# A recurrence with chunked preparation: ScalarE's copy of the decay product moves behind the scan, preparation is spread anew, and all preparations of the prologue stand ahead of the turning of the inverse

## The chip, the cores and the metric

The kernel runs on one core of one Trainium2 chip, in one launch. The metric is the device time of a launch in microseconds (us). An engine executes its own instructions strictly in the order in which the program gives them, and waits at an instruction until what it reads is there. So where an instruction stands in an engine's order is as much a part of the kernel as what it computes.

## What is computed

The first part is a linear recurrence for 32 heads (4 batches of 8) over 768 time steps, with a state of 40 x 40 for each head. The second part is a small mixture of attention experts that reads the recurrence's output `x`.

```
for t in range(768):                                  # state: (4, 8, 40, 40), zero at first
    y[t]  = einsum('bhd,bhde->bhe', r[t], state)
    Sa    = einsum('bhde,bhe->bhd', state, a[t])
    state = state * w[t][:, :, None, :] - einsum('bhd,bhe->bhde', Sa, b[t])
    state = state + einsum('bhd,bhe->bhde', v[t], k[t])
x = y as (4, 768, 320)
# for each of 4 experts: q, k, v = x @ wq, x @ wk, x @ wv; causal softmax attention; @ wo;
# out += (the expert's gate, if it is one of the token's two best) * that
```

All tensors are float32; `w` lies between 0.85 and 0.95.

## The kernel before, in words

**Tiling.** The 768 steps are cut into 24 chunks of 32 steps. The heads are cut into 4 groups of 8. A unit is one chunk of one group, so there are 96 units. Four chunks make a block (the code's `w` or `W`, 0 to 5), that is 16 units.

**Preparation.** For every block and group there is one preparation (`prep(i)`, i = 4W + group, 0 to 23), on tiles of 104 partitions. Its parts have one-letter names, and the tables that set the order use them:
- `a`: VectorE scans the decays backward, which gives their products from each step to the chunk's end (tile SUF, L248; the odd ones of groups 1 to 5 go to a part of TT).
- `b`: ScalarE copies four of these products, the decay over the whole stretch, to PC (L250). They are needed much later, when the state crosses into the next block (L413).
- `c`, `s`: VectorE's reciprocal (L252) and its second, forward scan (SC, L254).
- `x`: a multiply that gives AA (L256). `k`, `l`: VectorE's two multiplies that give KB (L261); `p` is the same on GpSimd in one instruction (L258), and only the prologue uses it.
- `m`, `n`: 32 small matmuls each on TensorE (L275) and the masked evacuation to GL by VectorE (L278). `o`: the DMA that puts a part of GL into DRAM (Ld, L282).
- `d`, `q`: AA copied into GL, by ScalarE for the first eight preparations, by VectorE for the others (L265, L267).
- `w`, `v`, `e`: the loads of the next preparation's inputs into EW, EA, EK.

**Inverse.** Each block needs the inverse of triangular matrices of 32 x 32 (`invert`): `L` loads them from Ld to MT, `C` sets the diagonal, `T5` does five of the elimination's instructions (L309), `A`, `B`, `D`, `E` turn the result by VectorE's transpose into TT (L311). It runs on GpSimd, 60 instructions a block. For block 0 it runs on VectorE with 28 instructions in the prologue (`T28`), then `P` turns a part into P1 (L313), and `F0`, `H0` to `F3`, `H3` finish it on TensorE and ScalarE, one chunk at a time (L320, L328).

**The loop.** It has 100 steps n, each with seven places in a fixed order: `u` of unit n-1 (L382, L384), `g` of unit n (L373, L376), `y` of unit n-3 (the state product, L405, L415; on VectorE at a block's end, L413), `f` of unit n-2 (L395, L398), `t` (L431, L435), `k` (L362, L366), `v` of unit n-1 (L389, L390). The decay multiply of the step (L419) stands behind the jobs of the place `f`. A unit's chain goes from TensorE to ScalarE or VectorE and back at each place, and its state is needed again four steps later by the same group.

**What sets the order.** START is the prologue, ahead of the loop. EARLY, SIDE, SIDE2 and INV add jobs to the loop's steps: the key is the step relative to 16(W-1), and the slashes count the seven places, so that `"///0abc"` puts a, b and c of the block's group 0 behind place 3, `f`. SIDE2 stands in for SIDE for block 2, which starts three steps later because EARLY still finishes block 1 in the first steps. In the kernel before, START prepares groups 0 to 4 fully and groups 5 and 6 in part ahead of `T28`; the parts of 5 to 7 that are left stand behind `F0` or in EARLY.

**Buffers.** In the prologue the inputs of preparations 1 to 7 lie in tiles that the loop needs only later (E8). SUF is one tile, so a next scan overwrites it only when `b`, `p` or `k`, `l` of the one before have read it.

Of the kernel before, what the change touches and what calls it, by code (L numbers as in the profile page):

```python
# [22 lines left out]
EARLY = {
    0: "///6cs",
    1: "5mno///6x 7apb/F1",
    2: "6mno///7csx/H1",
    3: "7mno E8",
    4: "/F2/5d/5q",
    5: "/H2/6d/6q",
    6: "/F3/7d/7q",  # L30
    7: "/H3",
}

SIDE = {
    -16: "///0abc",
    -15: "///0sx///0wv",
    -14: "///0k",
    -13: "///0l 1abc///0e",
    -12: "///0m 1s///1w",
    -11: "///1xkl///1ve",  # L40
    -10: "///2abc 1m",
    -9: "///2sx///2wv",
    -8: "///2kl///2e",
    -7: "///3abc 2m",
    -6: "///3sx///3wv",
    -5: "///3k",
    -4: "///3l 0ndqo///3e",
    -3: "///3m 1ndqo",
    -2: "///2ndqo",
    -1: "///3ndqo",  # L50
}

SIDE2 = {
    -13: "///0abc",
    -12: "///0sx///0wv",
    -11: "///0kl 1abc///0e",
    -10: "///1sx///1wv",
    -9: "///0m 1kl///1e",
    -8: "///2abc 1m",
    -7: "///2sxk///2wv",  # L60
    -6: "///2l 3abc///2e",
    -5: "///2m 3sx///3wv",
    -4: "///3kl 0ndqo///3e",
    -3: "///3m 1ndqo",
    -2: "///2ndqo",
    -1: "///3ndqo",
}
# [903 lines left out]
```

## Time and profile before

| what | value |
|---|---|
| median of 3 runs | 684.5 us (683.43 to 689.24) |
| the profiled execution's own time | 682.19 us |
| its span in the profile | 680.0 us |
| TensorE matmul, busy | 593.9 us (87%) |
| VectorE (DVE), busy | 493.1 us (73%) |
| ScalarE (ACT), busy | 474.3 us (70%) |
| GpSimd (POOL), busy | 321.0 us (47%) |

PE is TensorE's matmul and PEld its weight load. A time like 218.06 is counted from the span's start. In the rows of the timeline the first number is the start, the second the duration of the row's instructions together, and the bracket behind gives how long the engine sat idle just before and what ended that. Whole-span shares hide stages with different limits, so the stretches of the recurrence are looked at one by one. The first state product of chunks 4, 8, 12, 16 and 20 starts at 152.9, 215.1, 278.8, 337.6 and 379.6 us; these are the stretches' borders.

### The profile page before, as it was taken

To read this page: it belongs to the slowest core of one execution; us is meant where nothing else is said; L and a number is where in the kernel's file an instruction comes from. 1 tells how busy PE (TensorE), PEld (TensorE's weight loads), DVE (VectorE), ACT (ScalarE), POOL (GpSimd) and SP (SyncE) were. 2 spreads that over 40 slices of the span, in tenths; PEclk is the share of its full clock that TensorE was granted. 3 is DMA by queue.
4 is the path that set the end of the run, shared out by engine and by line. 5 is a ranking of instruction groups with operands and counts; after the bars stand their busy time and mean duration, and the time that the engine had idled before them with its cause. 6 is when DMAs were issued, how large, how long until landed. Compare 5 with 4: busy or idle time off the path is not lost. (4 is left out here: it accounts for less than half of the span.)

```text
span 680.0 us, 23382 instructions
## 1 busy us (share of the span) xinstructions
PE 593.9 (87%) x9361; PEld 514.6 (76%) x9361; DVE 493.1 (73%) x1164; ACT 474.3 (70%) x1295; POOL 321.0 (47%) x456
## 2 busy tenths in 40 slices
PE   5538797987997998889999989889899989999995
PEld 5527686976886887778988777778778877887774
DVE  7687458787887788788757776668887587667651
ACT  6892376666876786778899998457576666676762
POOL 2312089529925980797286020135555255343731
PEclk8555659788899799899999999989999999999998
DMA  7750445445655455653633882522131213202101
GB/s 240 221 124 11 105 126 120 103 119 151 153 128 157 129 135 115 181 131 87 174 97 83 259 211 69 165 56 73 56 92 35 78 32 83 65 11 57 40 30 46
DMA packets 63693, 73.90 MB, mean 109 GB/s; under 512 B 30168, under 2 KB 48344, under 8 KB 63576
## 3 DMA queue, kind: packets, MB, share of 16 engines
q1 hardware_dynamic: 63432, 72.21, 40.5%
q8 instruction: 77, 1.26, 0.8%
q14 instruction: 40, 0.33, 0.2%
q10 hardware_dynamic: 144, 0.10, 0.0%
HBM read 54.99 MB, written 11.01 MB: 97 GB/s over the span
## 5 line engine op out<-in xcount | busy, mean ns | idle before, releaser
L820 POOL TENSOR_TENSOR P<-P,m 128x128 f32<-128x128 f32 (+2 forms) x96 | 87.6, 934 | 95.3 <-DVE m L816 49.4
L309 POOL TENSOR_TENSOR MT<-MT,TP 128x30 f32<-128x30 f32 (+9 forms) x150 | 97.6, 651 | 11.8
L405 PE MATMUL py<-R,LS 128*40 128x80 f32 x1536 | 89.9, 246 | 14.9 <-ACT LS L435 9.7
L309 POOL TENSOR_TENSOR TP<-MT 128x30 f32<-128x30 f32 (+9 forms) x150 | 93.6, 624 | 11.4
L398 DVE TENSOR_TENSOR R<-ps,CM 64x128 f32<-64x128 f32 x192 | 55.1, 287 | 45.7 <-PE ps L395 42.2
L405 PEld LDWEIGHTS py<-R,LS 128*40 128x40 f32 x1536 | 67.4, 124 | 24.3 <-ACT LS L435 16.5
L809 ACT ACTIVATE P<-sc,m 128x128 f32<-128x128 f32 (+2 forms) x96 | 60.8, 634 | 29.9 <-DVE m L808 23.5
L275 PE MATMUL ps<-AA,KB 40*64 40x32 f32 x1536 | 64.2, 244 | 19.4 <-DVE AA L256 14.0
L275 PEld LDWEIGHTS ps<-AA,KB 40*64 40x64 f32 x1536 | 60.3, 164 | 23.0 <-issue 18.7
L808 DVE TENSOR_REDUCE m<-sc 128x1 f32<-128x128 f32 (+2 forms) x96 | 59.4, 622 | 20.1 <-PE sc L801 18.8
L798 PE MATMUL sc<-ks,qs 128*128 128x384 f32 (+4 forms) x256 | 62.5, 345 | 5.3 <-ACT P L809 5.1
L376 ACT ACTIVATE GT<-ps 32x160 f32<-32x160 f32 x192 | 56.4, 294 | 14.2 <-PE ps L373 10.8
L395 PE MATMUL ps<-RB,VU 128*64 128x64 f32 x768 | 49.3, 238 | 13.7 <-ACT VU L390 13.5
L384 ACT ACTIVATE R<-ps 32x160 f32<-32x160 f32 x192 | 56.6, 295 | 5.4 <-PE ps L382 1.2
L395 PEld LDWEIGHTS ps<-RB,VU 128*64 128x64 f32 x768 | 39.1, 148 | 19.5 <-ACT VU L390 18.5
L828 PE MATMUL pt<-CM,P 128*128 128x128 f32 x336 | 51.9, 276 | 2.1 <-ACT pt L834 1.8
L366 ACT ACTIVATE LS<-pt 64x320 f32<-64x320 f32 x96 | 41.4, 432 | 15.9 <-PE pt L362 14.5
L435 ACT ACTIVATE LS<-pt 40x320 f32<-40x320 f32 x92 | 39.6, 430 | 15.7 <-PE pt L431 12.6
L382 PE MATMUL ps<-GT,TT 128*33 128x80 f32 x768 | 48.8, 252 | 1.8 <-ACT GT L376 0.9
L798 PEld LDWEIGHTS sc<-ks,qs 128*128 128x128 f32 x256 | 40.8, 190 | 10.5 <-ACT P L809 9.4
L720 PE MATMUL pt<-xh,wq 128*128 128x384 f32 x192 | 43.3, 361 | 2.8 <-DVE pt L832 1.2
L431 PE MATMUL pt<-CM,R 104*104 104x104 f32 x368 | 44.6, 266 | 0.2 <-issue 0.2
(154 smaller groups left out, 1314.0 us busy)
## 6 DMA issues: line engine op xcount, KB each, us to landing
RB<-in_RB SPq DMA_DIRECT2D x24, 320.0 KB
EK<-in_EK SPq DMA_DIRECT2D x18, 416.0 KB
ks<-ks SPq DMA_DIRECT2D x32, 192.0 KB
R<-in_VG SPq DMA_DIRECT2D x24, 208.0 KB
EA<-in_EA SPq DMA_DIRECT2D x19, 208.0 KB
EW<-in_EA SPq DMA_DIRECT2D x18, 214.5 KB
R<-in_VT SPq DMA_DIRECT2D x48, 80.0 KB
R<-in_RT SPq DMA_DIRECT2D x24, 160.0 KB
```

The costliest lines, as they stand in the source:

```text
L275: T.matmul(p_a[64 * s:64 * s + 64, p, cc - c], kb[q, n, :], aa[q, n, :], start=True, stop=True, tile_position=(64 * s, 64 * s))
L309: return [lambda: e.tensor_tensor(tmp, row, col, op=OP.mult), lambda: e.tensor_tensor(o, o, tmp, op=OP.add)]
L376: A.activation(gt[b:b + 32, s::2], p_g[64 * s:64 * s + 32], AF.Copy)
L384: A.activation(hd(r2[32:64, 40 * h0:40 * h0 + 320], 80)[:, x::2], p_u[64 * x:64 * x + 32], AF.Copy, scale=-1.0)
L395: T.matmul(p_f[64 * x:64 * x + 64, y], vu[:, p, :], rb[:, 4 * g + p, :], start=True, stop=True, tile_position=(0, 64 * x))
L398: V.tensor_tensor(o[:, :, x], p_f[64 * x:64 * x + 64], mask[x][:, None, None, :].to_broadcast([64, 2, 2, 32]), op=OP.mult)
L405: T.matmul(py[64 * s:64 * s + 40, p], ls[:, h, :], m, start=True, stop=True, tile_position=(0, 64 * s))
L798: T.matmul(ps[:, c, 0:cw], QS[b][:, e, o], KS[b][:, e, z, k], start=(z == 0), stop=(z == 1 and not last), skip_group_check=True)
L808: V.tensor_reduce(m[:, 0, t:t + 1], ps[:, 0:ch, 0:cw], axis=AX.XY, op=OP.max, negate=True)
L809: later(DE, lambda: A.activation(pv, ps[:, 0:ch, 0:cw], AF.Exp, bias=m[:, 0, t:t + 1], accum_out=m[:, 1, t:t + 1]))
L820: PL.tensor_tensor(P[:, 0:n], P[:, 0:n], m[:, 3, t:t + 1].to_broadcast([128, n]), op=OP.mult)
L828: T.transpose(p[:, 128 * y:128 * y + 128], st["P"][t][:, 128 * c:128 * c + 128], ident)
```

## The change

- START is written anew. All eight preparations of blocks 0 and 1 stand ahead of `A B P F0 H0`. Their `m n o` stand behind the next group's `a` (and for groups 0 to 2 behind `csx` of the next as well), and `b` stands some way behind `a` and not right after it. Preparation 1 makes KB on VectorE. `T28` is cut into two `T14` with group 7's `m n o` between them.
- EARLY keeps `F1` to `H3` alone, at other steps.
- SIDE has `b` two or three steps behind `a`, at most three parts of a preparation in a step, and the copies `d q` are taken out of steps -4 to -1 and put into steps 1, 3, 6 and 8, when the block before runs. SIDE2 and INV1 are gone: all blocks use SIDE and INV. INV starts `C` and `T5` in the step of `L`.
- RB1 and P1 no longer have memory of their own; they lie in TT of block 1. Input tiles of preparation 7 lie elsewhere, and its SUF is the one in TT.

```diff
-START = """Z0 E4 0abcsxkl E5 E7 E6 1apb 0m 0d 0q 0n 0o 1csx W2 2apb 1m 1d 1q 1n 1o W4 2csx 3apb 2m 2d 2q 2n 2o W0 W1 V00 V10
-3csx 4apb 3m 3d 3q 3n 3o L W3 4csx W5 W6 5apbc 4m 4n C V01 V11 k0 g0 4o Z1 4d 4q T28 A B P F0 5s H0 5x 6apb"""
+START = """Z0 E4 0acsxklb E5 E7 E6 1acsxkl W2 0d 0q 1b 2ap 0mno 2csx W4 1d 1q 2b 3ap 1mno 3csx W0 2d 2q 4ap W1 3b 2mno 3mno L W3 V00 V10 3d 3q
+4csx W5 W6 5ap C 4b 4mno V01 V11 5csx Z1 4d 4q 6ap 5b 5mno k0 g0 6csx 5d 5q 7ap E8 6b 6mno 7csx T14 7mno 7b 6d 6q T14 A B P F0 H0 7d 7q"""
 SIDE = {
-    -16: "///0abc",
-    -15: "///0sx///0wv",
-    -4: "///3l 0ndqo///3e",
+    -16: "///0ac",
+    -15: "///0s///0w",
+    -14: "///0bx///0v",
+    -12: "///1acs///1w",
+    -1: "///2no 3mno",
+    1: "///0dq",
-SIDE2 = {
-INV = {0: "L", 1: "C T5", 2: "T5", 3: "T5", 4: "T5", 5: "T5", 6: "T5", 7: "T5", 8: "T5", 9: "T5", 10: "T5///A", 11: "T5", 12: "T5", 14: "///D", 16: "E"}
+INV = {0: "L C T5", 1: "T5", 2: "T5", 3: "T5", 4: "T5", 5: "T5", 6: "T5", 7: "T5", 8: "T5", 9: "T5", 10: "T5///A", 11: "T5", 14: "///D", 16: "E"}
-    RB1 = [ep.tile([128, 8, 32], F32, name=f"RB1{k}") for k in range(2)]
-    P1 = ep.tile([128, 32, 16], F32, name="P1")
+    RB1 = [TT[1][:, 8 * k:8 * k + 8] for k in range(2)]
+    P1 = TT[1][:, 16:32].rearrange("k n t -> k (n t)").rearrange("k (n r) -> k n r", r=16)
-        SUF = SUFs[1 if i in (1, 3, 5) else 0]
+        SUF = SUFs[1 if i in (1, 3, 5, 7) else 0]
```

Line numbers of the changed kernel are 16 lower behind the tables (L250 becomes L234, L275 becomes L259), and 15 lower at a few places ahead.

VectorE in the prologue, from the scan `a` of preparation 2 on. In the kernel before, the evacuations L278 of a group stand between its neighbour's scan L248 and that neighbour's L252, L254, L256:

```order
L248 SCALAR_TENSOR_TENSOR SUF_85<-SC_97,D_80 104x528
L278 TENSOR_TENSOR GLe<-ps,CM 64x4x2x32 x4
L252 RECIPROCAL D1P_84<-SUF_85 104x4
L254 SCALAR_TENSOR_TENSOR SC_93<-SC_97,D1P_84 104x528
L256 TENSOR_TENSOR AA_110<-LS_124,SC_93 104x512
L248 SCALAR_TENSOR_TENSOR TT_121<-R_128,D_80 104x528
L278 TENSOR_TENSOR GLe<-ps,CM 64x4x2x32 x4
```

The changed kernel, from the same scan on (L232 is the scan, L262 the evacuation):

```order
L232 SCALAR_TENSOR_TENSOR SUF_85<-SC_97,D_80 104x528
L262 TENSOR_TENSOR GLe<-ps,CM 64x4x2x32 x4
L236 RECIPROCAL D1P_84<-SUF_85 104x4
L238 SCALAR_TENSOR_TENSOR SC_93<-SC_97,D1P_84 104x528
L240 TENSOR_TENSOR AA_110<-LS_120,SC_93 104x512
L232 SCALAR_TENSOR_TENSOR TT_117<-R_124,D_80 104x528
L262 TENSOR_TENSOR GLe<-ps,CM 64x4x2x32 x4
L236 RECIPROCAL D1P_84<-TT_117 104x4
L238 SCALAR_TENSOR_TENSOR SC_93<-R_124,D1P_84 104x528
L240 TENSOR_TENSOR AA_111<-R_124,SC_93 104x512
L232 SCALAR_TENSOR_TENSOR SUF_85<-SC_96,D_80 104x528
L262 TENSOR_TENSOR GLe<-ps,CM 64x4x2x32 x8
```

The rows read alike, but the evacuations now belong to the group before: behind the scan of preparation 2 stand those of group 0, not 1, and the last row holds those of groups 2 and 3.

TensorE around the inverse of block 0, before (L275 are the matmuls of `m` and `n`, L320 and L328 those of `F0` and `H0`, L382 is `u` of the first unit):

```order
L275 MATMUL ps<-AA_108,KB_102 64x32 x32
L362 MATMUL pt<-CM,KB_98 128x104 x4
L373 MATMUL ps<-R_125,GLe 33x40 x8
L320 MATMUL ps<-P_118,TT_121 32x16 x32
L328 MATMUL ps<-TT_121,RB_116 32x16 x32
L382 MATMUL ps<-GT_135,TT_121 33x80 x4
L275 MATMUL ps<-AA_109,KB_103 64x32 x32
L373 MATMUL ps<-R_125,GLe 33x40 x8
```

and after the change (L259, L304, L312, L366):

```order
L259 MATMUL ps<-AA_109,KB_103 64x32 x32
L346 MATMUL pt<-CM,KB_98 128x104 x4
L357 MATMUL ps<-R_121,GLe 33x40 x8
L259 MATMUL ps<-AA_110,KB_104 64x32 x32
L259 MATMUL ps<-AA_111,KB_105 64x32 x32
L304 MATMUL ps<-TT_118,TT_117 32x16 x32
L312 MATMUL ps<-TT_117,TT_118 32x16 x32
L366 MATMUL ps<-GT_131,TT_117 33x80 x4
L357 MATMUL ps<-R_121,GLe 33x40 x8
```

The matmuls of groups 5, 6 and 7 moved from behind the first unit's `u` to ahead of `F0`.

ScalarE in the loop, around the PC copy of preparation 13 (block 3's second group), before:

```order
L384 ACTIVATE R_127<-ps 32x2x80 x2
L376 ACTIVATE GT_138<-ps 32x4x40 x2
L415 ACTIVATE R_126<-py_77 40x4x40 x2
L250 ACTIVATE PC_86<-SUF_85 104x4
L366 ACTIVATE LS_123<-pt 64x320
L366 ACTIVATE LS_124<-pt 64x320
L390 ACTIVATE VU_129<-ps 80x256
```

and after the change:

```order
L368 ACTIVATE R_124<-ps 32x2x80 x2
L360 ACTIVATE GT_133<-ps 32x4x40 x2
L399 ACTIVATE R_122<-py_78 40x4x40 x2
L234 ACTIVATE PC_86<-SUF_85 104x4
L419 ACTIVATE LS_120<-pt 40x8x40 x2
L374 ACTIVATE VU_126<-ps 80x256
```

The copy stands at the same kind of place, but in a later step: n = 38, where the scan that it reads stands in step 36; before, copy and scan both stand in step 35.

## Rows read from the trace of the kernel before

**Rows 1.** Stretches (busy us of PE, PEld, DVE, ACT, POOL; PE clock; DMA share; GB/s).
```profile
0.00:55.70 55.70, 26.39 (x565) 25.22 (x565) 42.00 (x87) 42.52 (x57) 13.09 (x16) 0.62 0.64 179
55.70:75.50 19.80, 19.06 (x414) 17.56 (x416) 12.05 (x20) 5.34 (x18) 3.90 (x2) 0.50 0.09 16
75.50:152.90 77.40, 65.65 (x1439) 58.80 (x1435) 54.30 (x112) 49.72 (x146) 44.12 (x73) 0.78 0.51 124
152.90:215.10 62.20, 54.95 (x1193) 48.98 (x1187) 50.07 (x107) 47.11 (x142) 40.14 (x60) 0.95 0.55 140
215.10:278.80 63.70, 56.28 (x1190) 50.26 (x1185) 50.78 (x109) 46.13 (x140) 40.27 (x61) 0.92 0.57 140
278.80:337.60 58.80, 53.41 (x1196) 47.52 (x1190) 47.12 (x104) 46.47 (x140) 38.64 (x60) 0.97 0.55 137
337.60:379.60 42.00, 41.99 (x937) 37.18 (x933) 26.56 (x83) 38.66 (x113) 28.40 (x55) 1.00 0.41 116
```
**Rows 2.** Waits, 75.5 to 152.9: who waited for whom, us, times, longest us.
```profile
ACT PC L250 <- DVE SUF L248: 14.9, 5, 4.4
```
**Rows 3.** Waits, 152.9 to 215.1.
```profile
ACT PC L250 <- DVE SUF L248: 7.4, 4, 2.6
```
**Rows 4.** Waits, 215.1 to 278.8.
```profile
ACT PC L250 <- DVE SUF L248: 7.1, 4, 2.4
```
**Rows 5.** Waits, 278.8 to 337.6.
```profile
ACT PC L250 <- DVE SUF L248: 4.8, 3, 2.4
```
**Rows 6.** Timeline of all engines, 217.5 to 221.6, around preparation 13's scan.
```profile
218.06 1.36 DVE L248 TENSOR_TENSOR_SCAN SUF<-EW,D 104x528 f32<-104x528 f32 x1
...
219.46 0.21 ACT L250 ACTIVATE PC<-SUF 104x4 f32<-104x4 f32 x1 [2.39 <-DVE SUF L248]
...
220.58 0.38 ACT L390 ACTIVATE VU<-ps 80x256 f32<-80x256 f32 x1
...
221.01 0.45 PE L395 MATMUL ps<-RB,VU 128*64 128x64 f32 x8 [2.60 <-ACT VU L390]
...
221.51 0.28 DVE L398 TENSOR_TENSOR R<-ps,CM 64x128 f32<-64x128 f32 x1 [1.55 <-PE ps L395]
```
**Rows 7.** Timeline of VectorE in the prologue, 22 to 30: scans of preparations 3 and 4.
```profile
22.80 1.25 DVE L248 TENSOR_TENSOR_SCAN TT<-R,D 104x528 f32<-104x528 f32 x1
...
29.71 1.25 DVE L248 TENSOR_TENSOR_SCAN SUF<-SC,D 104x528 f32<-104x528 f32 x1
```
**Rows 8.** VectorE's waits, 8 to 30.
```profile
DVE GLe L278 <- PE ps L275: 5.2, 5, 1.7
```
**Rows 9.** Timeline of TensorE, 52 to 57: F0 and the first `u`.
```profile
52.36 1.05 PE L320 MATMUL ps<-P,TT 16*32 16x16 f32 x64 [10.31 <-DVE P L313]
...
55.70 0.75 PE L382 MATMUL ps<-GT,TT 128*33 128x80 f32 x8 [0.76 <-ACT TT L329]
```
**Rows 10.** TensorE by line, 55.7 to 75.5 (form, count, busy us, mean ns, idle before).
```profile
L275 PE MATMUL ps<-AA,KB 40*64 40x32 f32 x192 | 10.9, 292 | 0.7 <-DVE AA L256 0.7
```
**Rows 11.** VectorE by line, 190 to 210, while GpSimd is busy for 2.4 us.
```profile
L267 DVE COPY GL<-AA 40x512 f32<-40x512 f32 x8 | 3.4, 423 | 0.2
...
L261 DVE TENSOR_TENSOR KB<-EK,SUF 104x512 f32<-104x512 f32 x1 | 0.7, 694 | 0.0
```
**Rows 12.** VectorE by line, 147 to 190, while GpSimd is busy for 38.4 us.
```profile
L261 DVE TENSOR_TENSOR KB<-EK,SUF 104x512 f32<-104x512 f32 x7 | 6.1, 898 | 0.1
```
**Rows 13.** Timeline of ScalarE: the PC copy of preparation 5.
```profile
44.01 0.21 ACT L250 ACTIVATE PC<-TT 104x4 f32<-104x4 f32 x1
```
**Rows 14.** ScalarE's waits, 4 to 44.
```profile
ACT PC L250 <- DVE TT L248: 3.7, 2, 1.9
...
ACT PC L250 <- DVE SUF L248: 1.2, 1, 1.2
```
**Rows 15.** Timeline of VectorE: the first instruction of block 0's inverse.
```profile
41.43 0.19 DVE L309 TENSOR_TENSOR TP<-MT 128x28 f32<-128x28 f32 x1
```
**Rows 16.** GpSimd's costliest group, from the page (form, count, busy us, mean ns, idle).
```profile
L309 POOL TENSOR_TENSOR MT<-MT,TP 128x30 f32<-128x30 f32 (+9 forms) x150 | 97.6, 651 | 11.8
```

More of the change, by code (lines that the diff above doesn't have):

```diff
@@ L23 @@
 EARLY = {
[L24 to L31, printed above, removed]
+    1: "////F1",
+    2: "////H1",
+    4: "////F2",
+    5: "////H2",
+    7: "////F3",
+    8: "////H3",
 }
 SIDE = {
-    -16: "///0abc",
-    -15: "///0sx///0wv",
[L37 to L46, printed above, removed]
-    -4: "///3l 0ndqo///3e",
-    -3: "///3m 1ndqo",
-    -2: "///2ndqo",
-    -1: "///3ndqo",
-}
-SIDE2 = {
[L54 to L67, printed above, removed]
@@ L68 @@
-INV = {0: "L", 1: "C T5", 2: "T5", 3: "T5", 4: "T5", 5: "T5", 6: "T5", 7: "T5", 8: "T5", 9: "T5", 10: "T5///A", 11: "T5", 12: "T5", 14: "///D", 16: "E"}
-INV1 = {4: "L", 5: "C T5", 6: "T5", 7: "T5", 8: "T5", 9: "T5", 10: "T5", 11: "T8", 12: "T8///A", 13: "T8", 14: "T8", 15: "///D", 16: "E"}
+    -16: "///0ac",
+    -15: "///0s///0w",
+    -14: "///0bx///0v",
+    -13: "///0kl///0e",
+    -12: "///1acs///1w",
+    -11: "///1x 0m///1v",
+    -10: "///1bkl///1e",
+    -9: "///2ac 1m",
+    -8: "///2s///2w",
@@ L72, in layouts @@
+    -7: "///2bxk///2v",
+    -6: "///2l///2e",
+    -5: "///3ac 2m",
+    -4: "///3s 0no///3w",
+    -3: "///3bx 1no///3v",
+    -2: "///3kl///3e",
+    -1: "///2no 3mno",
+    1: "///0dq",
+    3: "///1dq",
+    6: "///2dq",
+    8: "///3dq",
+}
+INV = {0: "L C T5", 1: "T5", 2: "T5", 3: "T5", 4: "T5", 5: "T5", 6: "T5", 7: "T5", 8: "T5", 9: "T5", 10: "T5///A", 11: "T5", 14: "///D", 16: "E"}
 def layouts(r, k, v, w, a, b):
@@ L152, in recurrence @@
     MT = ring("MT", [128, 32, 32], 2)
-    RB1 = [ep.tile([128, 8, 32], F32, name=f"RB1{k}") for k in range(2)]
-    P1 = ep.tile([128, 32, 16], F32, name="P1")
-    EA7 = ep.tile([104, 512], F32, name="EA7")
     TP = sp.tile([128, 240], F32, name="TP")
@@ L174, in recurrence @@
     E8 = [own, thirds(r20), (flat(SC[11]), flat(LS[1])[:, 0:512], g1[:, 0:1024]), thirds(r21),
-          (flat(SC[8]), flat(XT[1][:, 4:8]), flat(KB[8])), (flat(SC[9]), flat(XT[1][:, 0:4]), flat(KB[9])), own, (flat(SC[10]), EA7, flat(TT[1]))]
+          (flat(SC[8]), flat(XT[1][:, 4:8]), flat(KB[8])), (flat(SC[9]), flat(XT[1][:, 0:4]), flat(KB[9])), own, (flat(SC[10]), flat(LS[1])[:, 512:1024], flat(XT[0]))]
     SUFs = SUF, flat(TT[0])[0:104, 0:529]
@@ L454, in recurrence @@
         inv = invert(W)
-        for r, line in (SIDE if W != 2 else SIDE2).items():
+        for r, line in SIDE.items():
             if W == 1:
@@ L460, in recurrence @@
                     at(n0 + r, k, *[P[4 * W + int(z[0])][x] for x in z[1:]])
-        for r, line in (INV1 if W == 1 else INV).items():
+        for r, line in INV.items():
             for k, part in enumerate(line.split("/")):
```

## The prediction

> **What bounds the kernel now.** I read the table of stretches first [rows 1]. The stretch from 337.6 to 379.6 us holds 16 units with no preparation beside them: 42.0 us, TensorE busy for all of it at a granted clock of 1.00, which is 2.4 GHz. The three stretches ahead of it hold 16 units each and a preparation of four groups, and take 62.2, 63.7 and 58.8 us. No engine fills them: TensorE is busy for 53 to 56 us at a mean clock of 0.92 to 0.97 (a mixture of 1.2 and 2.4 GHz), VectorE for 47 to 51, ScalarE for 46 to 47. So about 12 us of each are lost to engines that wait for one another. The first stretch, 75.5 to 152.9, takes 77.4 us and VectorE is busy for 54.3.
>
> Then I read the waits. In all four stretches ScalarE's PC copy waits for the scan: 14.9, 7.4, 7.1 and 4.8 us [rows 2 to 5]. The timeline shows what one such wait does [rows 6]: the scan begins at 218.06, ScalarE stands at PC for 2.39 us until 219.46, its next VU copy comes at 220.58, TensorE has waited 2.60 us for that VU and VectorE 1.55 us for TensorE's product. So a copy of 0.21 us that nobody needs soon stops the unit's chain on three engines.
>
> In the prologue, the scans of preparations 3 and 4 begin 6.91 us apart [rows 7], and VectorE waits 5.2 us for the `m n` matmuls by then [rows 8]. Behind F0 the first `u` stands at 55.70 [rows 9], but the first state product comes only at 75.5 us; of these 19.8 us TensorE spends 10.9 on the `m n` of groups 5 to 7 [rows 10].
>
> **Part 1: `b` moved behind the scan (loop).** The copy stays, the wait goes, because in the new order the scan stands at least two steps ahead of its copy. What the copy would delay now is only the next scan, which comes two or more steps later. Taken at its plain length the wait gives 7.4, 7.1 and 4.8 us. A gain above that is possible: TensorE's stop at 221 is followed by matmuls at the lower clock, and the mean clock of these stretches is under 1.00 [rows 1]. A gain below it is possible too, because VectorE's work stays and takes 47 to 51 us of each stretch. I take the plain length: 54.8, 56.6 and 54.0 us. The floor is the larger of VectorE's busy time and TensorE's; for TensorE that is 42.0 plus the matmuls of four groups, four thirds of 10.9 at the low clock or 14.5, halved at the high one, about 7: 49. So the floor is about 50, 51 and 49.
>
> **Part 2: the spreading.** The same instructions stand in more steps, so this costs and gives nothing by itself, except for `d q`. These eight copies of 0.42 us leave steps in which GpSimd is idle [rows 11] and go beside the inverse. The nearest row for such a move is KB's multiply: 694 ns with GpSimd idle and 898 ns beside it [rows 11, 12], so 1.3 times; eight copies would cost 8 x 0.13 = 1 us a stretch. Against that, `x` and `k l` of the last group move into the idle steps and win about as much (3 x 0.2). I take nothing, and 0 to 3 us for the range. Block 2's preparation has 16 steps and no longer 13. INV starts one step earlier; GpSimd waits there for its load anyway, and 16 steps of 3.4 us are longer than the 40 us of the inverse [rows 1].
>
> **Part 3: the prologue.** I follow VectorE, which has the most to do.
> - Scan 4 begins at 29.71 now. Of this the 5.2 us of waiting go, since `m n` now stand one group later; one pair `m n` fewer stands ahead of it (-1.8, four of 0.42 and their gaps), and KB of preparation 1 is added (two multiplies of 0.65: +1.3). So scan 4 begins at 24.0.
> - Scan (1.3), `m n` of 2 and 3 (3.6) and `c s x` (2.2) bring scan 5 to 31.0. From here on `m n` follow their own `x` again, as now, so a group costs 6.9 us: scan 6 would begin at 37.9.
> - But scan 6 overwrites what the PC copy of preparation 4 reads, and that copy now stands on ScalarE behind all the zeroing W0 to W6. ScalarE does the same instructions now ahead of its PC copy at 44.01 [rows 13], with 4.9 us of waits [rows 14] that go, and one more copy: 39. So scan 6 begins at 39.2, 1.3 late.
> - While it waited, the matmuls finished, so this group takes 5.1: scan 7 at 44.4, and the last `x` at 51.3.
> - From the inverse's first instruction [rows 15] to F0 [rows 9] it takes 10.9 us now, and 1.8 for group 7's `m n` in the middle: F0 at 64.0. From F0 to `u` 3.3 as now: 67.3 against 55.70, 11.6 later.
> - From `u` to the first state product, the 10.9 us of `m n` are gone: 19.8 - 10.9 = 8.9, so 76.2 against 75.5.
>
> SyncE's queue holds one wait more than a plain load, at `L` for the DMAs of group 3's `o`. Behind it stand the loads for `g0` and the first `f`; between `L` and the first `T14` lie some 20 us of the chain above, so I cost it at nothing; without that cover, `T14` would wait for it.
>
> So the prologue gives nothing (+0.7). If ScalarE's fill or group 7 stalls more, it is up to 9 late (one more group's 6.9 and 2 for PC); if the pattern of 5.1 holds for groups 5 to 7, up to 4 early.
>
> **Part 4: the first stretch.** It loses its 14.9 us of PC waits [rows 2]: 62.5. The preparation of block 2 is now spread over all 16 steps, and VectorE's work was 54.3. I take 61, between 56 and 65. RB1, P1 and preparation 7's inputs in shared tiles cost nothing that I can find: the next writer of each comes behind F3 and H3 or behind `x` of preparation 7.
>
> **Sum.** +0.7, -16.4, -7.4, -7.1, -4.8: -35.0. The span falls from 680.0 to 645, the profiled time from 682.2 to 647.2. The median of the runs is 684.5, 2.3 above that execution: 649.5, so I say 650.
>
> **A rule weighed.** The AA copies take 0.42 us each while GpSimd is idle [rows 11], and no row shows one beside the inverse. The Trainium skill, page "SBUF — State Buffer", section "Who interferes with whom", states that such a copy can take the port pair that VectorE and GpSimd share, and that then whichever of the two starts second is blocked until the other ends. Rows 11 and 12 agree in kind, 898 against 694 ns, for a multiply. By the rule the time is that of rival 1.
>
> **Rivals.**
> - *Rival 1, VectorE becomes the bound.* With the waits gone, VectorE is the engine with the most work left at 50 us, in lumps of up to three parts in a step, and each AA copy stands up to one GpSimd instruction (0.65 us [rows 16], 8 x 0.65 = 5.2) in a queue. For it: 47 to 51 us of work, three engines near 50 and a strict order. Against it: without the waits the second stretch leaves (62.2 - 7.4) / 16 = 3.4 us a step, and VectorE needs 50 / 16 = 3.1. The stretches then take 65, 59.5, 60.5 and 57: -20.1 and +0.7, so 665.
> - *Rival 2, the floors are reached.* The clock stays at 2.4 GHz and the stretches take 57, 52, 53 and 51: -49.1 and +0.7, so 636.
> - *Rival 3, the preparations are only put in line (slower).* The three groups moved ahead of F0 cost three full periods of 6.9, or 20.7, while `u` to the first state product still takes 19.8, because it was the chain's latency and not `m n` that filled it. The four stretches keep their length except for half the first one's PC waits, 7.5: +13, so 698. It makes the kernel slower from a first state product at 75.5 + 7.5 = 83 us on, if the stretches gain no more than that. Against it: the matmuls of [rows 10].
> - *Rival 4, nothing changes.* What the PC wait held back is held back by the next wait in the chain (VU behind the scan's lump on VectorE), and only the first stretch gains what the prologue loses: within 7 us of 684.
>
> **How the numbers follow.** Forecast 0.66 (range of its own 640 to 660), rival 1 0.20, rival 2 0.06, rival 3 0.03, rival 4 0.05. 8 in 10 lie between 638 and 668: nearly all of the forecast and most of rival 1. About 1% is what a measurement of this kernel can tell from no change. The forecast and rivals 1 and 2 are all faster by more than that: 0.92; within 1%: 0.05; slower: 0.03.
>
> **What would show it.** In the changed profile the wait of PC for SUF is under 1 us in each stretch, the first state product comes at 72 to 80 us, the four stretches take 61, 55, 57 and 54 us at clocks near 1.00, and the rest is as before (42 and 300 us). PC waits gone with stretches near 60 mean rival 1; a first state product behind 85 us means that Part 3 is wrong; PC waits that stay mean that VectorE lags by two steps.

## The result and the profile after

The changed kernel takes 652.6 us (median of 4 runs, 647.4 to 657.3) against 686.1 us (median of 4 runs, 683.4 to 689.2): a ratio of 0.948, 95% interval 0.941 to 0.956. The execution that was profiled took 647.4 us with a span of 645.6; the span of before was 680.0.

The table of stretches after the change, cut at the first state product of chunks 0, 4, 8, 12, 16 and 20 as [rows 1] are (a stretch, its length, then busy us of PE, PEld, DVE, ACT and POOL with their instructions, the granted TensorE clock, DMA share and GB/s):

```profile
0.00:67.00 67.00, 34.91 (x730) 33.43 (x733) 55.52 (x109) 44.99 (x61) 17.70 (x23) 0.62 0.68 176
67.00:75.90 8.90, 8.37 (x262) 7.66 (x255) 1.83 (x4) 6.61 (x19) 7.77 (x15) 0.50 0.12 32
75.90:134.30 58.40, 54.05 (x1441) 48.46 (x1438) 45.85 (x99) 46.96 (x144) 31.92 (x49) 0.99 0.54 133
134.30:190.50 56.20, 52.06 (x1187) 46.30 (x1185) 50.97 (x108) 46.51 (x140) 38.69 (x58) 1.00 0.63 156
190.50:247.80 57.30, 52.42 (x1191) 46.41 (x1187) 51.08 (x108) 46.83 (x142) 41.66 (x64) 1.00 0.64 154
247.80:302.70 54.90, 51.64 (x1189) 46.02 (x1186) 48.42 (x106) 45.55 (x137) 39.05 (x59) 1.00 0.58 146
302.70:344.80 42.10, 42.09 (x938) 37.32 (x931) 30.48 (x89) 38.67 (x113) 29.68 (x57) 1.00 0.43 120
344.80:645.60 300.80, 276.53 (x2483) 229.22 (x2477) 210.07 (x547) 198.32 (x545) 112.47 (x134) 0.98 0.28 78
```

Against [rows 1] the span is 34.4 us shorter: the first state product comes +0.4 later (75.5 to 75.9), the four stretches change by -19.0, -6.0, -6.4 and -3.9, and what is behind them by +0.5. In the four stretches TensorE now runs at a mean clock of 0.99 to 1.00 (0.78 to 0.97 before) and is idle for 3.3 to 4.9 us in each of them.

TensorE's idle time and its busy time both became shorter. In the last three stretches together its idle time falls from 20.1 to 12.3 us, and its busy time from 164.6 to 156.1 us with nearly the same matmuls (x3579 and x3567). So of the 16.3 us won there, 7.8 are idle time and 8.5 go with the higher clock, which was 0.92 to 0.97 there. In the first stretch, 7.4 of the 19.0 us are idle time and 11.6 are busy time, again with the same matmuls (x1439 and x1441).

The longest waits of the second stretch, 134.3 to 190.5 (engine, tile and line <- what it waited for: us in total, times, longest us):

```profile
POOL MT L279 <- DVE GL L251: 13.1, 1, 13.1
ACT LS L350 <- PE pt L346: 5.6, 4, 2.8
DVE R L382 <- PE ps L379: 2.2, 3, 0.9
PEld py L389 <- ACT LS L419: 1.5, 5, 0.4
```

The row of PC (L234) for SUF, 7.4 us in [rows 3], is gone here and in the other three stretches. What is left on ScalarE is mainly a wait for TensorE's transposes, and GpSimd's 13.1 us are the pause between two inverses.

### The profile page after: what moved, and what is told of

It reads as the page before. It is cut to its first block, busy times and chain, and to the rows that moved or that the text cites. A ratio compares the mean times of both kernels' runs of the same rounds, so it can differ in the third digit from the quotient of the medians.

```text
span 645.6 us, 23402 instructions
## 1 busy us (share of the span) xinstructions
PE 572.1 (89%) x9361; PEld 494.8 (77%) x9361; DVE 494.2 (77%) x1166; ACT 474.4 (73%) x1295; POOL 318.9 (49%) x455
## 3 DMA queue, kind: packets, MB, share of 16 engines
q8 instruction: 77, 1.26, 0.8%
## 5 line engine op out<-in xcount | busy, mean ns | idle before, releaser
L293 POOL TENSOR_TENSOR MT<-MT,TP 128x30 f32<-128x30 f32 (+9 forms) x150 | 97.5, 650 | 11.8
L293 POOL TENSOR_TENSOR TP<-MT 128x30 f32<-128x30 f32 (+9 forms) x150 | 93.7, 625 | 11.4
L389 PE MATMUL py<-R,LS 128*40 128x80 f32 x1536 | 86.2, 237 | 6.7 <-issue 2.8
L382 DVE TENSOR_TENSOR R<-ps,CM 64x128 f32<-64x128 f32 x192 | 54.9, 286 | 33.3 <-PE ps L379 29.6
L259 PE MATMUL ps<-AA,KB 40*64 40x32 f32 x1536 | 60.5, 238 | 20.4 <-DVE AA L240 12.6
L389 PEld LDWEIGHTS py<-R,LS 128*40 128x40 f32 x1536 | 63.8, 118 | 16.5 <-ACT LS L419 6.8
L259 PEld LDWEIGHTS ps<-AA,KB 40*64 40x64 f32 x1536 | 57.0, 157 | 23.4 <-issue 18.9
L368 ACT ACTIVATE R<-ps 32x160 f32<-32x160 f32 x192 | 56.6, 295 | 4.9 <-PE ps L366 0.8
L379 PE MATMUL ps<-RB,VU 128*64 128x64 f32 x768 | 47.0, 228 | 2.7 <-ACT VU L374 2.5
L366 PE MATMUL ps<-GT,TT 128*33 128x80 f32 x768 | 46.4, 242 | 1.9 <-ACT GT L360 0.9
L419 ACT ACTIVATE LS<-pt 40x320 f32<-40x320 f32 x92 | 39.6, 430 | 10.8 <-PE pt L415 7.6
L830 PE MATMUL ot<-pt,vv 128*64 128x256 f32 (+1 forms) x384 | 43.5, 359 | 0.0
L415 PE MATMUL pt<-CM,R 104*104 104x104 f32 x368 | 42.4, 258 | 0.0
```

The costliest lines, as they stand in the source:

```text
L259: T.matmul(p_a[64 * s:64 * s + 64, p, cc - c], kb[q, n, :], aa[q, n, :], start=True, stop=True, tile_position=(64 * s, 64 * s))
L293: return [lambda: e.tensor_tensor(tmp, row, col, op=OP.mult), lambda: e.tensor_tensor(o, o, tmp, op=OP.add)]
L368: A.activation(hd(r2[32:64, 40 * h0:40 * h0 + 320], 80)[:, x::2], p_u[64 * x:64 * x + 32], AF.Copy, scale=-1.0)
L382: V.tensor_tensor(o[:, :, x], p_f[64 * x:64 * x + 64], mask[x][:, None, None, :].to_broadcast([64, 2, 2, 32]), op=OP.mult)
L389: T.matmul(py[64 * s:64 * s + 40, p], ls[:, h, :], m, start=True, stop=True, tile_position=(0, 64 * s))
L830: T.matmul(po[h, 128:256] if one else po[h], VV[b][:, k, 2 * ep + s], P[:, 256 * k:256 * k + (128 if one else 256)], start=(k == 0), stop= ...
```

## The experiments

Each experiment that is timed has its own runs of before on the same chip, so kernels that ran on different chips are compared by their ratio to it. That has a limit of its own: one kernel that ran on two chips (e7 and e12 below) had 0.937 (0.932 to 0.943) on one and 0.947 (0.943 to 0.951) on the other. Differences under 1% are therefore read only between kernels that ran together.

**e1: `b` alone, in the kernel before.** Only the PC copies move, one or two steps behind their scan, in SIDE and SIDE2:

```diff
-    -16: "///0abc",
+    -16: "///0ac",
-    -14: "///0k",
-    -13: "///0l 1abc///0e",
+    -14: "///0bk",
+    -13: "///0l 1ac///0e",
...
```

> The kernel before with one edit: in the loop's tables the PC copy b of each preparation of blocks 2 to 5 stands one to two steps behind its scan; prologue, spreading and copies d q are as before. Theory W (the PC waits are lost time, each at its plain length): the waits 14.9, 7.4, 7.1 and 4.8 us go from the four stretches, so they take about 62.5, 55, 56.5 and 54 us and the span falls by 34, from 680 to about 646, as much as the whole change gave. Rival S (the scan's lump on VectorE stops the chain, and ScalarE only shows it): f waits for VectorE in place of PC, the four stretches fall by less than 2.5 us each and the span stays above 670; the gain then comes from the spreading.

Measured: 668.1 us, ratio 0.973 (0.964 to 0.982), 18.6 us of 687.3 (12 to 25). PC waits for nothing any more in the four stretches, yet the stretches are 69.8, 57.8, 57.1 and 57.1 us: the last three get only 12.7 us shorter, of the 19.3 us of PC waits that they had. Some other waits are longer now. From the second stretch (147.5 to 205.3), three waits and the row of the stretch:

```profile
ACT LS L435 <- PE pt L431: 5.4, 5, 3.2
PE ps L275 <- DVE KB L261: 2.0, 1, 2.0
DVE KB L261 <- DMA EK<-in_EK: 1.6, 1, 1.6
147.50:205.30 57.80, 53.95 (x1189) 47.89 (x1186) 49.46 (x108) 46.65 (x141) 41.27 (x63) 0.97 0.64 152
```

The first of them was 2.1 us before; KB now reaches its EK load before it has landed, which was no wait before; TensorE's wait of `m n` for KB was 1.7 us before. Neither theory is right as written: the wait goes, but about two thirds of its length are won in these three stretches. That the old spread of the preparation is the reason isn't shown. TensorE is idle for 11.4 us of e1's last three stretches, no longer than after the whole change (12.3). What they are longer by, 172.0 against 168.4 us, is TensorE's busy time at a mean clock of 0.97 against 1.00, and another execution of the whole change (e5 below) takes 173.4 us for the three.

**e2: the kernel after with `b` right behind `a` again in SIDE.**

```diff
-    -16: "///0ac",
+    -16: "///0abc",
-    -14: "///0bx///0v",
+    -14: "///0x///0v",
...
```

> The changed kernel with one edit undone: in the loop b stands right behind a again; spreading and prologue stay new. Theory W: four waits of 1 to 2.5 us come back in each of four stretches, about 7 us each, so the stretches take about 65, 63, 64 and 60 us and the span about 672, against 645.6. Rival S: with the work spread, VectorE reaches the scan early, the waits are under 1 us each and the span stays under 655.

Measured: 671.3 us, ratio 0.974 (0.966 to 0.983). The PC wait is back in all four stretches, 3.8, 8.0, 8.1 and 5.0 us, and they take 63.1, 64.5, 65.2 and 62.8 us. The second stretch, 139.0 to 203.5: its two longest waits behind GpSimd's pause, and its row of the stretches:

```profile
ACT PC L234 <- DVE SUF L232: 8.0, 4, 2.6
DVE R L382 <- PE ps L379: 7.0, 7, 2.4
139.00:203.50 64.50, 57.77 (x1191) 51.80 (x1186) 51.45 (x108) 46.95 (x142) 41.88 (x68) 0.89 0.54 136
```

VectorE's wait for the matmuls of the place `f` goes from 2.2 to 7.0 us with it, and the clock from 1.00 to 0.89. This profiled execution was the slowest of its four and that of after the fastest of its four, so the size is better read from the ratios: 0.974 less 0.948 is 2.6% of 687, or 18 us, for waits of 24.9 us. By the two intervals it can be anything from 10 to 26 us. e5's profiled execution was the slowest of its four too: against it, TensorE's idle time in e2's last three stretches is 18.8 and not 10.8 us, and its busy time 173.7 and not 162.6. So in these two executions the PC waits go with more of both, idle time and time at the lower clock (0.89 to 0.90 against 0.94 to 0.97); why the clock falls more often with them isn't shown.

**e3: the prologue alone.** START, EARLY and the tiles of the kernel after, with the old SIDE and INV for all blocks.

> The changed kernel's prologue, tiles and early steps with the loop tables of before for all blocks (b right behind a, d q in steps -4 to -1, INV as before). Theory W with Part 3 of the prediction: the first state product stays at 75 to 77 us, the later stretches stay at about 62, 63 and 59, and the first stretch takes about 65 (the waits of a full table, 7, stay in it, but those that the late load of preparation 8 and the leftovers of block 1 made, some 8, go, and the table starts three steps earlier): span about 668. Rival S: the prologue by itself gives nothing or loses, span 675 to 690.

Measured: 673.3 us, ratio 0.978 (0.970 to 0.987), 15.1 us of 687.3 (9 to 21). The first two rows of its stretches:

```profile
75.90:141.70 65.80, 58.94 (x1439) 53.01 (x1436) 48.34 (x105) 46.52 (x141) 32.74 (x50) 0.89 0.47 115
141.70:204.70 63.00, 56.07 (x1189) 50.14 (x1186) 50.71 (x109) 46.17 (x140) 42.12 (x65) 0.92 0.56 141
```

The first state product stays at 75.9, as in after, and stretches 2 to 4 keep their old length (63.0, 63.3, 59.6). The gain lies in the first stretch: 77.4 to 65.8, while `b` stands where it stood. Its PC wait is 7.9 us there; it was 14.9 [rows 2]. With the old SIDE for all blocks, block 2's preparation also gets 16 steps in place of 13, so the run shows the new prologue and this together. Between the two profiled executions the span differs by 9.1 us, and 15 is the value from all runs.

e1 and e3 together give 2.7% + 2.2% = 4.9%. The whole change gives 5.2%. So, if the two simply add, the spreading of the loop's preparation brings 0.3% beside them, less than the intervals.

**e4: the copies `d q` back at steps -4 to -1.**

```diff
-    -4: "///3s 0no///3w",
+    -4: "///3s 0ndqo///3w",
...
-    1: "///0dq",
-    3: "///1dq",
-    6: "///2dq",
-    8: "///3dq",
```

> The changed kernel with the copies d q alone put back into steps -4 to -1, beside an idle GpSimd. Theory W with Part 2: the copies take 0.42 us there in place of 0.69, which gives VectorE back 1.7 us a stretch, but they stand in a row with n o; the span stays within 4 us of 645.6. Rival: the spreading of d q is what smooths the stretch, and the span rises by 3 us in each of four stretches to about 658.

Measured: 657.3 us, ratio 0.956 (0.947 to 0.965), where after has 0.948 (0.941 to 0.956). The stretches are 61.8, 56.6, 56.7 and 57.6 us, against 58.4, 56.2, 57.3 and 54.9. The second and third are as in after; the first and last are longer by about 3 us, with mean clocks of 0.89 and 0.94, but so they are in another execution of after itself (62.7 and 57.6, e5 below). Whether `d q` at steps 1 to 8 gain anything is not settled: the difference of the ratios is 0.8%, with an uncertainty of 1.2%.

**e5 to e8 ran together.** e5 is the kernel after again.

> The kernel after, unchanged, beside the next three runs on one chip, so that each of them can be compared with it. 652 us expected, within 5.

Measured: 655.2 us (649.7 to 658.3), ratio 0.948 (0.943 to 0.954). Its profiled execution took 658.3 us, with stretches of 62.7, 58.5, 57.3 and 57.6, so it shows what separates executions of one kernel. One place of the second stretch, counted from the stretch's border, first in e5, then in the execution of after that is shown above:

```profile
148.00:154.90 6.90, 4.84 (x115) 4.13 (x113) 6.61 (x15) 6.24 (x19) 6.27 (x9) 1.00 0.82 179
154.90:162.00 7.10, 7.09 (x96) 6.75 (x97) 4.65 (x11) 3.02 (x9) 6.39 (x10) 0.52 0.28 76
```
```profile
142.70:149.60 6.90, 4.91 (x115) 4.19 (x113) 6.64 (x14) 6.22 (x19) 6.27 (x9) 1.00 0.81 178
149.60:156.70 7.10, 6.75 (x150) 6.08 (x151) 6.80 (x14) 4.91 (x15) 6.47 (x9) 1.00 0.37 106
```

In e5 TensorE's clock falls to its lower level, 1.2 GHz, for 7 us, and three steps (from one state product to the next) take 5.7, 4.0 and 2.8 us where the other execution takes 4.2, 3.0 and 3.0: 2.3 us for one such dip. Ahead of it TensorE was busy for 4.84 of 6.9 us with 115 matmuls; in the other execution, with the same 115 matmuls and 4.91 us, no dip follows. So at this place the clock falls in some executions and not in others, and no row here tells why.

**e6: `m n o` of groups 4 to 6 one group later, and PC's copies of 4 and 5 ahead of ScalarE's zeroing.** It goes for the waits that the prologue still has (0.94 and 0.83 us for `m n` in two of three groups and 0.66 in the third, 0.98 for PC).

```diff
-4csx W5 W6 5ap C 4b 4mno V01 V11 5csx Z1 4d 4q 6ap 5b 5mno k0 g0 6csx 5d 5q 7ap E8 6b 6mno 7csx T14 7mno 7b 6d 6q T14 A B P F0 H0 7d 7q
+4csx 4b 5ap C W5 5csx 4mno V01 V11 5b 6ap W6 6csx 5mno Z1 4d 4q 6b 5d 5q k0 g0 7ap E8 7csx 6mno T14 7b 6d 6q 7mno T14 A B P F0 H0 7d 7q
```

> Prologue of the kernel after, with the m n o of groups 4, 5 and 6 one group later (behind the c s x of the next group) and the PC copies of preparations 4 and 5 ahead of the zeroing W5, W6, Z1 on ScalarE. The same instructions in another order; the loop is untouched. Theory L (the prologue is held up by waits: VectorE for TensorE's m n, 1.8 us for each of three groups, and scan 6 for the PC copy, 1 us): the first state product comes at about 70 instead of 75.9 us, the time falls by 5 to 6 us against the run of after. Theory B (VectorE's or TensorE's work fills the prologue and the waits only move, for instance to group 7's m n): first state product at 75 to 76, time within 1 us of after.

Measured: 657.0 us, ratio 0.951 (0.945 to 0.958), first state product at 76.8 us. The waits are gone and nothing is won. VectorE's timeline shows why, and GpSimd's beside it (start, us, engine and line, instruction):

```profile
33.09 3.13 DVE L238 TENSOR_TENSOR_SCAN SC<-SC,D1P 104x528 f32<-104x528 f32 x1
44.27 1.26 DVE L232 TENSOR_TENSOR_SCAN TT<-SC,D 104x528 f32<-104x528 f32 x1
45.78 2.83 DVE L238 TENSOR_TENSOR_SCAN SC<-SC,D1P 104x528 f32<-104x528 f32 x1
48.65 2.49 DVE L240 TENSOR_TENSOR AA<-LS,SC 104x512 f32<-104x512 f32 x1
32.92 2.19 POOL L242 TENSOR_TENSOR KB<-KB,TT 104x1024 f32<-104x1024 f32 x1 [4.99 <-DVE TT L232]
44.35 3.14 POOL L242 TENSOR_TENSOR KB<-EK,SUF 104x1024 f32<-104x1024 f32 x1
47.46 3.13 POOL L242 TENSOR_TENSOR KB<-XT,TT 104x1024 f32<-104x1024 f32 x1
```

The scan at 33.09 needs 1.26 us alone. It starts 0.17 behind GpSimd's KB and ends at 36.22, 1.11 behind KB's end at 35.11. At 44.3 it is the other way: the scan is first and KB takes 3.14 us in place of 2.19. Then the scan at 45.78 ends 1.12 behind that KB, and AA at 48.65 ends 0.55 behind the next. In the kernel after, the evacuations of `m n`, which read PSUM, stood beside KB, and they take their plain 0.88 us for two there. So part of VectorE's wait for `m n` cost nothing, by this reading: it lay where a scan would have been stopped.

**e7: `2no` a step earlier**, so that the step ahead of a block's border holds two `m n` parts and not three.

```diff
-    -2: "///3kl///3e",
-    -1: "///2no 3mno",
+    -2: "///3kl 2no///3e",
+    -1: "///3mno",
```

> The kernel after, with n and o of the third group moved from step -1 to step -2 in each loop preparation, so that the step before a block's border holds two TensorE parts (m n of the fourth group) instead of three. Theory P (the 5.6 us step comes from three m/n parts in one step on TensorE and VectorE): that step falls to about 4 us and step -2 grows by less than 1, stretches 2 to 4 lose about 1 us each, the time falls by 3 to 4 us. Theory S (the step is long because of what its unit's chain carries anyway): the stretches stay within 0.3 us.

Measured: 648.8 us, ratio 0.937 (0.932 to 0.943), 6.4 us under e5. The step of 5.6 us falls to 4.6, but the one ahead of it grows from 3.0 to 3.7, so the two together win 0.3 us, less than theory P says. Stretches at a clock of 1.00 take 55.5 us, where after has 54.9 to 57.3. The 6.4 us are more than these steps explain, and as e12 the same kernel had a ratio of 0.947, after's own. So a gain of this edit is not shown.

**e8: `d q` of blocks 2 to 5 left out** (the r and a columns of GL are not computed).

> The kernel after without the d and q copies of blocks 2 to 5 (eight copies a stretch, the r and a columns of GL; that part of the computation is left out). In the trace of after they take 6 x 691 + 2 x 424 ns = 5.0 us of VectorE's 51.0 us of work in the stretch from 134.3 to 190.5. Theory V (VectorE's work bounds the stretches now): the four stretches fall by 3.5 to 5 us each, the time by 14 to 20. Theory C (the units' chain over three engines at a granted clock of 1.00 bounds them, and VectorE has slack where the copies stand): under 1 us each, the time falls by less than 4.

Measured: 655.8 us, where e5 has 655.2. The first three stretches:

```profile
76.20:134.30 58.10, 55.75 (x1438) 50.35 (x1435) 45.62 (x97) 46.00 (x140) 31.92 (x50) 0.93 0.53 134
134.30:189.60 55.30, 52.16 (x1195) 46.33 (x1189) 45.47 (x100) 46.84 (x141) 37.81 (x58) 1.00 0.66 158
189.60:249.10 59.50, 56.09 (x1192) 50.26 (x1186) 45.53 (x100) 46.92 (x141) 38.95 (x62) 0.91 0.63 148
```

In the second stretch VectorE has 5.5 us less to do (45.47 against 50.97), the clock is 1.00 in both, and the stretch is 0.9 us shorter. The third is 2.2 us longer than after's with as much less work on VectorE, at a mean clock of 0.91. So VectorE's work is not the bound: theory C.

**e9 and e10: `m n` beside KB.** If the reading of e6 is right, the evacuations must stand where GpSimd's KB runs, each directly behind the scan `a` of the group two further on. e10 has e7's loop as well.

```diff
-START = """Z0 E4 0acsxklb E5 E7 E6 1acsxkl W2 0d 0q 1b 2ap 0mno 2csx W4 1d 1q 2b 3ap 1mno 3csx W0 2d 2q 4ap W1 3b 2mno 3mno L W3 V00 V10 3d 3q
-4csx W5 W6 5ap C 4b 4mno V01 V11 5csx Z1 4d 4q 6ap 5b 5mno k0 g0 6csx 5d 5q 7ap E8 6b 6mno 7csx T14 7mno 7b 6d 6q T14 A B P F0 H0 7d 7q
+START = """Z0 E4 0acsxklb E5 E7 E6 1acsxkl W2 0d 0q 1b 2ap 0mno 2csx W4 1d 1q 2b 3ap 1mno 3csx W0 2d 2q 4ap W1 3b 2mno 3d 3q 4csx 4b
+5ap W3 3mno L V00 V10 C W5 5csx 5b 6ap W6 V01 V11 4mno 6csx Z1 4d 4q 6b 7ap E8 5mno k0 g0 7csx 6mno 5d 5q T14 7b 6d 6q 7mno T14 A B P F0 H0 7d 7q
```

> Prologue of the kernel after with m n o of groups 3 to 6 one group later, as in e6, but each now directly behind the first scan of the group two further on, where GpSimd multiplies that group's KB (2.19 us); the loop is untouched. In e6 the waits for m n were gone, but the scan at 33.09 took 3.13 us and the one at 45.78 2.83 us instead of 1.26, and AA at 48.65 2.49 instead of 0.69, each ending with or behind a KB of GpSimd. Theory P (a VectorE operation with two inputs in SBUF and GpSimd's KB stop each other, one that reads PSUM is not stopped): with m n beside KB every scan takes 1.2 to 1.4 us and every AA 0.7, the last x of the prologue ends by 48 us (52.1 in after), the first state product comes at 72 us (75.9), the time falls by 3 to 4 us against after. Theory Q (the long scans came from something else, such as their tiles or the load traffic at that time): scans of 2.8 to 3.1 us stay, the first state product stays at 75 to 77.

> The prologue of e9 and the loop of e7 (n and o of the third group a step earlier). If the two gains add: the first state product at 72 us, stretches 2 to 4 at about 55.5 us where the granted clock stays at 1.00, 7 to 10 us below after, 642 to 645. If the prologue's gain is given back in the first stretch (its first steps wait for GpSimd's inverse of block 1 or for loads): the first state product at 72, the first stretch at 62 or above, 648 as in e7.

Measured: e9 652.6 us, ratio 0.947 (0.942 to 0.952); e10 648.5 us, 0.943 (0.938 to 0.947). In e9 all scans take 1.2 to 1.4 us, the last AA ends at 47.7 us, and the first state product comes at 73.4: theory P for the order. The 3 to 4 us of time that it forecast are not seen; the ratio is after's own (0.947 and 0.948, on two chips). One AA still takes 2.49 us, at 45.19. GpSimd's timeline names the reason:

```profile
41.77 0.15 POOL L279 MEMSET MT<- 128x32 f32 x1 [8.86 <-DMA MT<-Ld]
41.86 2.18 POOL L242 TENSOR_TENSOR KB<-EK,SUF 104x1024 f32<-104x1024 f32 x1
44.00 3.13 POOL L242 TENSOR_TENSOR KB<-XT,TT 104x1024 f32<-104x1024 f32 x1
```

`C`, a memset of 0.15 us that waits for the load of MT, stands ahead of KB of preparation 6 and holds both remaining KB. It is the same pattern as PC: a small operation that nobody needs soon, put in front of one that is needed. In e10, with the same prologue, the load came later still (11.6 us of waiting), VectorE then waited 2.3 us for the `m n` of group 6, and the first state product came at 75.8. So the two gains did not add there: 648.5 us, where 642 to 645 were expected if they did.

**e11: `C` behind the last KB, e10 otherwise; e12: e7 again, beside it.** The edit against e10 (the line goes on behind `5mno` as there):

```diff
-5ap W3 3mno L V00 V10 C W5 5csx 5b 6ap W6 V01 V11 4mno 6csx Z1 4d 4q 6b 7ap E8 5mno
+5ap W3 3mno L V00 V10 W5 5csx 5b 6ap W6 V01 V11 4mno 6csx Z1 4d 4q 6b 7ap C E8 5mno
...
```

> e10 with one job moved: GpSimd sets the diagonal of block 0's matrices (C, which waits for the load of MT) behind the KB of preparation 7 and no longer ahead of the KB of preparation 6. In e9 and e10 GpSimd stood 8.9 and 11.6 us at C, so that both KB came late, AA of group 7 took 2.49 us beside the last of them, and in e10 the m n of group 6 were waited for 2.3 us. If C is the cause: both KB run directly behind their scans, AA takes 0.7 us, the first state product comes at 71 to 72 us. If the first stretch keeps its length (60 to 61 us at e7's place), the time is 644 to 645, 4 below e12; if the first stretch gives the gain back (64 us), it is within 1 us of e12.

> e7 unchanged, beside e11 on the same chip: 648 us, within 4.

Measured: e11 647.0 us (641.0 to 648.9), ratio 0.939 (0.934 to 0.943); e12 651.9 us, 0.947 (0.943 to 0.951). Both KB now run behind their scans and no operation is stretched:

```profile
44.02 1.26 DVE L238 TENSOR_TENSOR_SCAN SC<-SC,D1P 104x528 f32<-104x528 f32 x1
45.31 0.69 DVE L240 TENSOR_TENSOR AA<-LS,SC 104x512 f32<-104x512 f32 x1
36.68 2.18 POOL L242 TENSOR_TENSOR KB<-EK,SUF 104x1024 f32<-104x1024 f32 x1 [3.53 <-DVE SUF L232]
41.97 2.18 POOL L242 TENSOR_TENSOR KB<-XT,TT 104x1024 f32<-104x1024 f32 x1 [3.11 <-DVE TT L232]
44.07 0.17 POOL L279 MEMSET MT<- 128x32 f32 x1
```

The first state product comes at 72.8 us, 3.2 ahead of e12's 76.0 and close to the 71 to 72 expected, and the time is 4.8 us under e12's. In the profiled executions 3.2 of it lie ahead of the first state product and 2.1 in the first stretch (59.4 against 61.5 us). The two kernels differ in the whole order of the prologue, so this is what the new order and `C` give together.

## Why the prediction was right, point by point

The time and the stretches of the gain came out as forecast: 650 against 652.6 us, a span of 645 against 645.6. How the time is won inside the stretches did not, as the points show. In the prologue the scans of preparations 4 to 7 start within 1 us of their working (24.0, 31.0, 39.2 and 44.4). VectorE's timeline of after (start, us, line, instruction, and in the bracket the idle time before it):

```profile
24.24 1.25 DVE L232 TENSOR_TENSOR_SCAN SUF<-SC,D 104x528 f32<-104x528 f32 x1
31.41 1.25 DVE L232 TENSOR_TENSOR_SCAN TT<-SC,D 104x528 f32<-104x528 f32 x1
39.39 1.26 DVE L232 TENSOR_TENSOR_SCAN SUF<-EW,D 104x528 f32<-104x528 f32 x1 [0.98 <-ACT PC L234]
45.24 1.25 DVE L232 TENSOR_TENSOR_SCAN TT<-SC,D 104x528 f32<-104x528 f32 x1
```

- **Part 1, `b` behind the scan.** The cause is right: e1 takes the PC waits out, e2 brings them back, and about 18 us go and come with them. The size "at plain length" is too large: forecast were 54.8, 56.6 and 54.0 us, measured 56.2, 57.3 and 54.9, or 16.3 of 19.3 us won. In e1 it is 12.7 of 19.3, in e5's execution 11.3, and in e2 18 us for 24.9 us of waits (10 to 26 by the intervals). And the sum took the wait itself as the loss. Of the 16.3 us only 7.8 are idle time of TensorE, and 8.5 are busy time, won with the clock at 1.00. The prediction named the clock as a possible gain on top of the plain length; it goes with half of what was won in this execution.
- **The floor in Part 1.** It put the `m n` of four groups at 7 us at the high clock, as half of 14.5. At a clock of 1.00 TensorE is busy for 52.06 us in the second stretch and for 42.09 in the one without a preparation, 10 us apart, and the `m n` alone are 8.6 of them. A group's 64 matmuls take 2.06 us at the high clock and 3.63 at the low one, 1.76 times and not twice. The rows stand below the list. The floor is thus 52 us, not 49, and TensorE is busy for 93% of the second stretch.
- **Part 2, the spreading.** It costs nothing that the runs can tell, as forecast, though the copies are dearer than forecast: six of them take 691 ns on average beside GpSimd, so the eight of a stretch cost 1.6 us more in VectorE's time, not 1. e8 shows that this time is not waited for. What else the new spread gives beside e1 and e3 is the 0.3% of above, which no run separates from nothing.
- **Part 3, the prologue.** Every step stands within about 1 us: scan 6 was late by 0.98 us behind PC (forecast 1.3), F0 came at 64.97 (64.0), the first `u` at 68.08 (67.3), and the first state product at 75.9 (76.2). What failed is the sentence "so the prologue gives nothing". By its border it gives nothing, and yet e3 measures it at 15 us (9 to 21), in the first stretch: VectorE's work there falls from 54.3 to 48.3 us in e3, and half of the PC waits go. TensorE's matmuls in that stretch stay the same (x1439 in both); its busy time falls from 65.7 to 58.9 us with the mean clock at 0.89 and no longer 0.78, and its idle time from 11.8 to 6.9.
- **Part 4, the first stretch.** Forecast 61 us and measured 58.4 (62.7 in e5's execution): the size is right, the working is not. It booked all 14.9 us of PC waits on `b`. Alone, `b` gives 7.6 us there (e1: 69.8) and the prologue 11.6 (e3: 65.8), and half of the PC waits go with the prologue. That the stretch loses 8.5 us of VectorE's work was not counted, and the two errors cancel. So the sum of the four stretches, forecast 226.4 us and measured 226.8, is closer than its parts deserve, and there is luck in it: in e5's execution of the same kernel the four take 236.1 us.
- **The rivals.** Rival 1 (VectorE becomes the bound) falls by e8. Rival 2 (636) needed stretches of 52 to 53, and TensorE's work alone is 52. Rival 3's case, a first state product behind 83 us, did not come. Rival 4 needed another wait in place of PC's; some waits did grow in e1, but of its 19.3 us 12.7 are won.

The rows for the floor in Part 1, from the profile after: the second stretch for L259 alone (busy us of PE and PEld), and one group's matmuls in the prologue at a granted clock of 1.00 and of 0.50:

```profile
134.30:190.50 56.20, 8.60 (x256) 7.96 (x256) 1.00 0.63 156
10.23 2.06 PE L259 MATMUL ps<-AA,KB 40*64 40x32 f32 x64
19.18 3.63 PE L259 MATMUL ps<-AA,KB 40*64 40x32 f32 x64 [2.34 <-DVE AA L240]
```

What bounds the stretches now is TensorE at its high clock, with 3.3 to 4.9 us of idle time, most of it at chain hand-overs. VectorE is excluded by e8; that it is TensorE is read from its busy time, and no run took TensorE work away to test it.

## What to carry to other kernels

A small operation that nobody needs soon costs its engine's whole queue if it stands in front of a wait; look for such rows (PC for SUF, `C` for MT) by the wait of a cheap instruction, and move the instruction behind what it waits for. Don't book the wait at its full length: here between about half and five sixths of it became time (18.6 us of 34.2 in e1, 16.3 of 19.3 in the last three stretches of after). Split a stretch's gain into idle and busy time of the engine that bounds it, because part of it can be the clock. Look also at which load or matmul is late next. A wait of one engine can be cover for a conflict with another, so a removed wait must be looked for again as a longer duration, and work that is moved ahead of a border must be counted in the stretch that it leaves.

## What the runs showed of the hardware

**VectorE and GpSimd stop each other over whole instructions.** e6 shows it for scans and KB, with the numbers above. In the loop of after, the copies `d q` show the same, each beside GpSimd's inverse in the first row and without it in the second (min/median/max ns, first and last start):

```profile
L251 DVE COPY GLe<-AA x6: 419/736/892, 136.3 to 154.9; 40x512 f32<-40x512 f32 x6
L251 DVE COPY GL<-AA x2: 422/424/425, 186.9 to 187.4; 40x512 f32<-40x512 f32 x2
```

The spread from 419 to 892 fits a wait for the rest of one GpSimd instruction (651 ns on average, [rows 16]). The Trainium skill, page "SBUF — State Buffer", section "Who interferes with whom", says that a VectorE instruction with two inputs in SBUF contends with a GpSimd instruction that reads SBUF, that one with at most one such input outside the two-port modes does not, and that for two-port modes the second starter is blocked for the whole instruction. The traces agree on scan, AA multiply and copy, and on the evacuations, which read one input from PSUM and were not stretched; e6's scans and multiplies show the whole-instruction block in both directions.

**TensorE stops in the middle of `H2`.** In the first stretch the 64 matmuls of L312 (32 x 16 outputs) are cut by an idle time that ends with "issue", that is, with nothing that the profile shows. It differs from execution to execution, and the step around it, from one state product to the next, goes with it: no stop and 4.9 us (e8), 0.4 and 5.4 (the profile after), 2.0 and 7.3 (e11), 2.1 and 7.9 (e5), 3.2 and 9.0 (e9), 3.4 and 9.2 (e12). The two rows of it in e7's timeline, and two stretches of e7 and after:

```profile
83.88 0.34 PEld L312 LDWEIGHTS ps<-TT,TT 32*32 32x32 f32 x32
83.89 0.43 PE L312 MATMUL ps<-TT,TT 32*32 32x16 f32 x31
...
86.72 0.62 PE L312 MATMUL ps<-TT,TT 32*32 32x16 f32 x33 [2.40 <-issue]
85.40:92.20 6.80, 5.23 (x92) 4.61 (x92) 1.63 (x5) 3.38 (x11) 6.09 (x10) 0.50 0.51 116
77.50:95.00 17.50, 16.39 (x542) 14.76 (x539) 15.07 (x30) 14.42 (x45) 16.01 (x20) 1.00 0.54 127
```

The stop goes together with a fall of the clock. In the nine profiled executions with a stop of 2 us or more at this place (e2, e4 to e7 and e9 to e12) TensorE's clock falls to 1.2 GHz during the stop or within about 2 us behind it, for 3 to 7 us; the last row but one is that of e7. After (0.4 us of stop, the last row) and e8 (none) stay at 2.4 GHz there. So the step loses more than the stop's own length. e3, with no stop here, is at the lower clock all the same, so the stop isn't the only thing that goes with it.

The span of e5's execution is 10.6 us over that of after: 1.1 ahead of the first state product, 4.2 in the first stretch, where this stop and the fall of the clock behind it stand, and 5.0 in the second and fourth, where the clock falls. What TensorE waits for stays open, and no run was made for it.
